# Delta-rule attention feeding a mixture of softmax attentions: scores and maxima as paired 64-row products

## The chip, the cores and the metric

The kernel runs on one core of one Trainium2 chip. The metric is the device time of one execution in microseconds. Three timed runs of the kernel before gave 500.80, 500.83 and 502.74 us, median 500.83. A separate execution was recorded by the profiler.

## The reference, cut to what matters

Inputs: q, k, v of shape 4 x 8 x 768 x 48 (batch, head, position, feature), beta, and weights for 4 experts with 64 features each. A first stage runs a delta rule over the positions of each batch and head:

```python
k_n = k / (norm(k) + 1e-6)
for t in range(768):
    y[t] = q[t] @ state
    state += beta[t] * outer(k_n[t], v[t] - k_n[t] @ state)
```

Its output, 4 x 768 x 384, is the input x of a causal softmax attention per expert, mixed with gates of the two best experts per position:

```python
for e in range(4):
    s = where(causal, -1e9, (x @ wq[e]) @ (x @ wk[e]).T / 8)
    a = exp(s - s.max(-1)); a /= a.sum(-1) + 1e-9
    out += gate[e] * (a @ (x @ wv[e]) @ wo[e])
```

## The kernel before, in words

The 768 positions are cut into three parts of 256, and the four batches into two pairs, which gives six stages n = 0..5: stages 0, 1, 2 walk along one pair of batches, 3, 4, 5 along the other. `s = n % 3` is the part. A stage has four chunks c of 64 positions, with 16 batch-head pairs side by side.

The delta rule of a stage is solved blockwise. `gram` (L214) forms products of the keys of a chunk; `solve_pre` and `solve_step` (L266, L311) invert triangular blocks of 32, or of 16 in stage 0, on VectorE (DVE) for stage 0 and on GpSimd (POOL) for the others, framed by the transposes of `st_in`, `st_out` and `st_nat`; the `merge` functions widen the blocks to 64. Then the chunks go one after another through `chain_ks`, `chain_u`, `chain_s`, `chain_q` and `chain_y` (L427 to L474). Their products are small and packed into quadrants of the array: the list `by` sorts the 16 pairs so that consecutive products use different row halves (r = 0 or 64) and column halves. `chain_q` (L459) reads rows r and writes partitions r; `chain_y` (L467) reads rows v and writes partitions r, where v is r or 64-r.

For the attention, `proj_qk` (L487) makes queries and keys of 128 positions for a pair of batches. Values are split into a high part, rounded to the type fp32r, and a low part with the rest. The tiles of 128 rows are laid out so that one product does two things. In `KA`, the half that belongs to a head's parity has the high part of the keys, the other half the low part; `QA` has the queries' high part in both halves. `KA * QA` is then khi*qhi + klo*qhi. In `KH`, one half has the keys' high part again, and eight rows of the other half hold -1 where a row belongs to expert e (`pick_rows`, L417); `QL` has the queries' low part and, in those eight rows, the row maxima (`max_rows`, L609). `KH * QL` is khi*qlo - max. For this each projection is copied out of PSUM by four ScalarE (ACT) copies of 64 x 512 (L508 and L511, or L508 and L514) and two DVE subtractions of 64 x 512 (L517 or L519).

`max_list` (L567) has units of one expert, or of two of the same parity: a product over up to 512 keys, a mask product in bf16 with an identity where the diagonal is reached, and a DVE maximum out of PSUM (L589). A score unit (`score`, L624) is one expert and two key blocks of 128: two products per block over 256 queries (128 for the last block of the diagonal), masks where kp = s, and exponentials on ACT into a tile of the pool `at` of five. `av` (L644) multiplies these with the values in column halves, into one of two places in the bank `PO`; ACT copies the 64 features and the row sum separately (L658, L659). `norm`, `fin_t` and `fin_o` scale, transpose and multiply with wo.

PSUM has eight banks: `po` one (also used by the filler), `xu` two, `py` two, and a ring of three named `pm_` for everything else.

What sets the order of the work is `ORDER` (L36), a list of steps that is played back as it stands; each engine's queue then runs in that order and waits on semaphores. `+39` in it is 39 fillers: products of 252 columns on a zero tile (L118) that keep TensorE busy. All loads, the spreading of rows (L480) and the stores are issued from SyncE (SP), in the same order. In the names of steps, gr is `gram`, gq `gram_q`, si `st_in`, pre and sv the solve, pj `proj_qk`, mx, mp and mr the maximum and its rows, sc `score`.

## Time and profile before

| what | value |
|---|---|
| median of three runs | 500.83 us |
| the profiled execution, whole | 500.28 us |
| its span, first to last instruction | 498.6 us |
| mean granted TensorE clock | 0.969 |
| instructions | 24842 |
| products on TensorE, each with its weight load | 11169 |
| the loading DMA queue's share of 16 DMA engines | 20.0% |

PE is TensorE's products, PEld its weight loads, which run beside them. Rows of the timeline give start, duration, engine, line, operation and tiles. `KA,QA` at L109 is a maximum's product, `QA,KA` and `QL,KH` are a score's; `mbias,identb` is a mask, `po<-zb` a filler. L109 is the line of the helper that issues every product. Rows that group instructions give count, busy time, mean duration in ns, and the idle time ahead of them with what ended it.

### The profile page before, as it was taken

How to read it: one execution, taken by the hardware profiler on the slowest of the kernel's cores; microseconds unless marked ns; L12 is line 12 of the kernel's file. 1: busy time of each engine (PE TensorE's matmuls, PEld its weight loads, DVE VectorE, ACT ScalarE, POOL GpSimd, SP SyncE). 2: the span in 40 equal slices, each digit the busy share in tenths (PEclk: the TensorE clock that was granted, in tenths of full speed). 3: DMA queues.
4: the chain of work that ended last, by engine and by line, in shares of the span. 5: the costliest groups of instructions: out<-in, count | busy, mean ns of one | idle time of the engine just before them, and what ended most of it. 6: DMA issues, size and time to landing. Idle time of an engine off the chain costs nothing.

```text
span 498.6 us, 24842 instructions
## 1 busy us (share of the span) xinstructions
PE 468.2 (94%) x11169; PEld 415.2 (83%) x11169; DVE 298.0 (60%) x661; ACT 264.0 (53%) x659; POOL 228.5 (46%) x382
## 2 busy tenths in 40 slices
PE   8998767899999999998989999999999999999997
PEld 6687657798899878887978899998898979988896
DVE  0479502246895887473797667676756863357522
ACT  3112352348566445645464556674566664773563
POOL 7101088683008885788711778625987020000000
PEclk9699975999999999999999999999999999999999
DMA  8500020424132210135301123013220112000002
GB/s 270 194 5 1 5 79 8 146 67 141 36 103 79 67 47 18 64 92 183 92 3 58 58 67 101 6 41 112 69 67 17 50 35 83 20 2 32 3 17 80
DMA packets 18825, 32.63 MB, mean 65 GB/s; under 512 B 2848, under 2 KB 8864, under 8 KB 18720
## 3 DMA queue, kind: packets, MB, share of 16 engines
q1 hardware_dynamic: 18720, 31.04, 20.0%
q8 instruction: 88, 1.44, 1.2%
q14 instruction: 17, 0.14, 0.1%
HBM read 23.96 MB, written 4.72 MB: 58 GB/s over the span
## 4 chain that ended last, share of the span: by engine, by line
PE 77%; DVE 10%; issue 5%; ACT 3%; SPq 3%; DMA 2%; ACTq 0%; DVEq 0%
PE po L109 15%; PE xu L109 7%; PE py L109 6%; SPq L480 2%; DVE mx L589 1%; DVE tt L346 1%; DMA xh<-h 1%; DVE tn L343 1%; DVE B L248 1%; DVE B L245 1%; DMA kf<-in_kq_dram 1%; DVE KA L517 1%; DVE QL L519 1%; ACT QA L511 0%; PE pm__3152 L109 0%
## 5 line engine op out<-in xcount | busy, mean ns | idle before, releaser
L324 POOL TENSOR_TENSOR B<-B,tm 128x30 f32<-128x30 f32 (+9 forms) x150 | 79.6, 530 | 11.8
L323 POOL TENSOR_TENSOR tm<-B 128x30 f32<-128x30 f32 (+9 forms) x150 | 73.7, 492 | 10.7
L109 PE MATMUL po<-zb 128*128 128x252 bf16 x385 | 53.3, 288 | 3.0 <-issue 1.4
L109 PE MATMUL po<-VS,at 128*64 128x65 f32 x1344 | 49.8, 226 | 0.1
L109 PEld LDWEIGHTS po<-VS,at 128*64 128x64 f32 x1344 | 43.1, 138 | 5.8 <-issue 1.9
L109 PEld LDWEIGHTS <-zb 128*128 128x128 bf16 x385 | 36.8, 102 | 10.3 <-issue 2.5
L141 POOL TENSOR_TENSOR kv<-kv,nt 128x384 f32<-128x384 f32 x24 | 19.9, 830 | 48.8 <-DMA kv<-in_kv_dram 19.3
L397 POOL MEMSET tt<- 32x1024 f32 x10 | 9.4, 944 | 50.1 <-PE pm__7779 L109 12.7
L658 ACT ACTIVATE os<-po 128x128 f32<-128x128 f32 x48 | 13.3, 278 | 26.8 <-PE po L109 26.5
L109 PEld LDWEIGHTS <-identb 128*128 128x128 bf16 x192 | 18.4, 96 | 7.6 <-issue 2.0
L109 PE MATMUL py<-qf,sb 48*48 48x64 f32 x704 | 24.6, 222 | 0.0
L301 POOL TENSOR_TENSOR B<-B,nn 128x1024 f32<-128x1024 f32 x5 | 11.8, 2369 | 27.7 <-DVE nn L300 27.7
L109 PEld LDWEIGHTS py<-qf,sb 48*48 48x48 f32 x704 | 21.8, 123 | 1.4 <-issue 0.4
L473 DVE TENSOR_TENSOR xh<-py,xh 112x384 fp32r<-112x384 f32 x24 | 13.4, 557 | 15.9 <-ACT h L472 15.7
L434 DVE TENSOR_TENSOR xs<-kv,xu 128x384 f32<-128x384 f32 x22 | 12.1, 551 | 15.8 <-PE xu L109 12.0
L471 ACT ACTIVATE xh<-py 112x384 fp32r<-112x384 f32 x24 | 11.8, 491 | 16.9 <-PE py L109 16.7
L452 DVE TENSOR_TENSOR sb<-sb,xu 112x384 f32<-112x384 f32 x20 | 11.0, 551 | 16.1 <-ACT at L639 7.3
L248 DVE STREAM_TRANSPOSE B<-tt 32x1024 f32<-32x1024 f32 x10 | 20.0, 2001 | 0.2
L440 ACT ACTIVATE ub<-xu 128x384 f32<-128x384 f32 x24 | 11.8, 490 | 13.6 <-PE xu L109 11.2
L109 PE MATMUL xu<-xs,tt 64*64 64x48 f32 x768 | 17.6, 225 | 1.4 <-issue 0.9
L109 PEld LDWEIGHTS xu<-xs,tt 64*64 64x64 f32 x768 | 14.6, 138 | 3.8 <-issue 1.7
L109 PE MATMUL py<-pm,ub 64*48 64x64 f32 x768 | 16.0, 221 | 0.6 <-issue 0.6
(2055 smaller groups left out, 1446.8 us busy)
## 6 DMA issues: line engine op xcount, KB each, us to landing
kv<-in_kv_dram SPq DMA_DIRECT2D x24, 384.0 KB, 3.6
kf<-in_kq_dram SPq DMA_DIRECT2D x24, 256.0 KB, 3.7
qf<-in_kq_dram SPq DMA_DIRECT2D x24, 256.0 KB, 3.7
out_dram<-ot SPq DMA_DIRECT2D x24, 192.0 KB, 1.9
xh<-h SPq DMA_DIRECT2D x72, 32.0 KB, 2.0
wst<-in_wqk_dram SPq DMA_DIRECT2D x3, 256.0 KB, 5.2
wst<-in_wvg_dram SPq DMA_DIRECT2D x1, 256.0 KB, 5.3
wst<-in_wo_dram SPq DMA_DIRECT2D x1, 256.0 KB, 3.5
```

Of the source, the lines that this page charges most:

```text
L109: T.matmul(o, lhsT=a, rhs=b, start=start, stop=stop, skip_group_check=True)
L141: G.tensor_tensor(vt, vt, PR[n]["nt"][:, c * NP:c * NP + NP, None].to_broadcast([128, NP, HD]), op=OP.mult)
L248: V.transpose(B[r:r + 32], gf[r:r + 32, :, 0:32].rearrange("p t j -> p j t"))
L301: G.tensor_tensor(pr["B"], pr["B"], nn[:, None, :].to_broadcast([128, 32, 32]), op=OP.mult)
L323: e.tensor_tensor(tv, bc(Z[:, i:i + 1, i + 1:]), bc(Z[:, 0:i, i:i + 1]), op=OP.mult)
L324: e.tensor_tensor(Z[:, 0:i, i + 1:], Z[:, 0:i, i + 1:], tv, op=OP.add)
L434: V.tensor_tensor(eight(XB), eight(vt), PX, op=OP.subtract)
L440: S.activation(eight(UB), PX, AF.Copy)
L452: V.tensor_tensor(eight(new), eight(state(n, c)), SP, op=OP.add)
L471: S.activation(hi, Y[:, :, 0:3], AF.Copy)
L473: V.tensor_tensor(lo, Y[:, :, 0:3], hi, op=OP.subtract)
L658: S.activation(os[:, :, e], O[:, :, 0:EH], AF.Copy)
```

## The change

Heads go through scores and maxima two at a time. `KHI`, `KLO`, `QHI` and `QLO` hold two experts in the two halves of the 128 rows, as they come out of the projection, so a projection takes one ACT copy and one DVE subtraction of 128 x 512. Every product of scores and maxima has 64 rows, and products of the two heads are issued in turn, each into a bank of its own. A score is khi*qhi + khi*qlo + klo*qhi and a fourth product of `SEL` (-1 in the rows of expert e) with `MR` (the row maxima); the maximum is taken of khi*qhi alone. Masks are two products of 64 rows per head. `score` and the units of the maximum take a pair of experts (y) and two banks, so there are half as many units.

The bank `po` is gone: fillers write to the unused half of a `py` bank, now with 256 columns, `av` takes a bank of the ring, and the ring has four banks (`bufs=4` wherever it had 3). `av` copies features and row sums at once, and `norm` writes to a new tile. The pool `at` has seven tiles (`ATB`). The queries have two buffers. The constants grow from 504 to 1012 columns and come in three DMAs instead of two. `ORDER` is a new list, with 250 fillers in place of 384. In the old one 88 fillers stand ahead of gr0.0, the last of the four gr0 steps, which si0 follows; in the new one all four gr0 steps come within 52 fillers, and si0 right behind them.

```diff
@@ ORDER, the first line of each
-+39 gr0.2 sq3 sq0 sq2 +12 gr0.1 +5 sr0 lc0.1 sq1 sr2 gr1.2 +3 sr1 +6 gq0.1 sr3 pre0.0 pre0.1 +1 gr1.0 pre0.2 w0 pre0.3
...
+sq1 +22 gr0.0 +9 gr0.2 sq2 +21 gr0.3 gr0.1 si0 lc0.1 sq3 sr1 gr1.1 sr2 sq0 +7 sr0 sr3 pre0.0 pre0.1 pre0.2 pre0.3
...
@@ -112,11 +104,11 @@
 
     ZB = cp.tile([128, 256], BF16, name="zb")
     V.memset(ZB, 0.0)
-    PO = ps.tile([128, 512], F32, name="po")
-    mm(PO[:, 260:512], ZB[:, 0:128], ZB[:, 0:252], True)
+    PY0 = ps.tile([128, 2, 512], F32, name="py")
+    mm(PY0[:, 0, 256:512], ZB[:, 0:128], ZB, True)
 
     def filler():
-        mm(PO[:, 260:512], ZB[:, 0:128], ZB[:, 0:252], False)
+        mm(PY0[:, 0, 256:512], ZB[:, 0:128], ZB, False)
 
     KR = [cp.tile([128, NP, 64], F32, name=f"kf{i}") for i in range(KB)]
     QR = [cp.tile([128, NP, 64], F32, name=f"qf{i}") for i in range(QB)]
...
@@ -144,18 +136,19 @@
 
     VS = cp.tile([128, 2, 6, NE, EH + 1], F32, name="VS")
     KF = VS.rearrange("p a b c d -> p (a b c d)")
-    cst = cp.tile([128, 240], F32, name="cst")
+    cst = cp.tile([128, 500], F32, name="cst")
     bta = cp.tile([128, NU, 32], F32, name="bta")
-    csb = wk.tile([128, 264], F32, name="csb", tag="at", bufs=5)
+    csb = wk.tile([128, 512], F32, name="csb", tag="at", bufs=ATB)
     load_k(0, 0)
-    nc.sync.dma_start(cst, consts[:, 0:240])
+    nc.sync.dma_start(cst[:, 0:240], consts[:, 0:240])
...
@@ -164,12 +157,15 @@
     pmask = cst[:, 128:192]
     lower = cst[:, 192:208]
     kmask = cst[:, 208:240]
-    identb = cp.tile([128, 128], BF16, name="identb")
-    mbias = cp.tile([128, 2, 128], BF16, name="mbias")
+    identb = cp.tile([128, 2, 128], BF16, name="identb")
+    mbias = cp.tile([128, 2, 2, 128], BF16, name="mbias")
     TG = [cp.tile([128, NT, 64], F32, name=f"tt{i}") for i in range(2)]
-    KA = cp.tile([128, NE, 2, NS], F32R, name="KA")
-    QL = cp.tile([128, NE, 2, 256], F32R, name="QL")
-    KH = cp.tile([128, NE, 2, NS], F32R, name="KH")
+
+
+    KHI = cp.tile([128, 2, 2, NS], F32R, name="KHI")
+    KLO = cp.tile([128, 2, 2, NS], F32R, name="KLO")
+    MR = cp.tile([128, 2, 2, 256], F32R, name="MR")
+    SEL = cp.tile([128, NE, 128], F32R, name="SEL")
 
     slot = lambda k, h: KF[:, 260 * k + 256 * h:260 * k + 256 * h + 256].rearrange("p (t i) -> p t i", t=NP)
     GO = [[slot(k, h) for k in ks for h in range(2)] for ks in ((0, 8), (4, 10))]
@@ -178,9 +174,8 @@
         G.memset(GO[0][c], 0.0)
     for t in AS + GO[1]:
         G.memset(t, 0.0)
-    for r, x in HA:
-        G.memset(QL[64 - r:128 - r, x::2].bitcast(F32), 0.0)
-        G.memset(KH[64 - r:128 - r, x::2].bitcast(F32), 0.0)
+    G.memset(SEL.bitcast(F32), 0.0)
+    G.memset(MR.bitcast(F32), 0.0)
 
     wqkh = cp.tile([128, 3, 512], F32R, name="wqkh")
     wqkl = cp.tile([128, 3, 512], F32R, name="wqkl")
...
@@ -411,14 +406,11 @@
         for w in LB:
             for r, _ in HA:
                 S.activation(w[r:r + 32, 0], ident[r:r + 32, r:r + 32], AF.Copy)
-        S.activation(identb, ident, AF.Copy)
-        S.activation(mbias.rearrange("p a b -> p (a b)"), csb[:, 0:256], AF.Copy)
+        S.activation(identb, cst[:, 240:496].rearrange("p (a b) -> p a b", a=2), AF.Copy)
+        S.activation(mbias.rearrange("p a h b -> p (a h b)"), csb, AF.Copy)
 
     def pick_rows(r, e):
-        S.activation(KH[64 - r:72 - r, e].rearrange("p b t -> p (b t)"),
-                     csb[64 - r:72 - r, 256 + e:257 + e].to_broadcast([8, 2 * NS]), AF.Copy)
-
-
+        S.activation(SEL[r:r + 8, e], cst[r:r + 8, 496 + e:497 + e].to_broadcast([8, 128]), AF.Copy)
 
     XH = {}
     first_of = lambda n, c: n % 3 == 0 and c == 0
@@ -488,10 +480,10 @@
         s = n % 3
         y, isk = m % 2, m // 2
         if n not in QT:
-            QT[n] = (wk.tile([128, NE, 2, 256], F32R, name="QA", bufs=1), QL)
+            QT[n] = tuple(wk.tile([128, 2, 2, 256], F32R, name=x, bufs=2) for x in ("QHI", "QLO"))
         xh = XH[n, hb][0]
         if y == 0:
-            PQ[0] = ps.tile([128, 2, 2, 128], F32, name="pm_", bufs=3)
+            PQ[0] = ps.tile([128, 2, 2, 128], F32, name="pm_", bufs=4)
         P = PQ[0]
         w = slice(128 * m, 128 * m + 128)
         j = 0
@@ -501,22 +493,10 @@
                 j += 1
         if y == 0:
             return
-        qa, ql = QT[n]
-        hs = [(slice(64 * x, 64 * x + 64), slice(64 - 64 * x, 128 - 64 * x), slice(x, NE, 2)) for x in range(2)]
+        hi, lo = (KHI, KLO) if isk else QT[n]
         t = slice(256 * s + 128 * hb, 256 * s + 128 * hb + 128) if isk else slice(128 * hb, 128 * hb + 128)
-        for h, _, es in hs:
-            S.activation((KA if isk else qa)[h, es, :, t], P[h], AF.Copy)
-        if not isk:
-            for h, o, es in hs:
-                S.activation(qa[o, es, :, t], P[h], AF.Copy)
-        else:
-            for h, _, es in hs:
-                S.activation(KH[h, es, :, t], P[h], AF.Copy)
-        for h, o, es in hs:
-            if isk:
-                V.tensor_tensor(KA[o, es, :, t], P[h], KA[h, es, :, t], op=OP.subtract)
-            else:
-                V.tensor_tensor(ql[h, es, :, t], P[h], qa[h, es, :, t], op=OP.subtract)
+        S.activation(hi[:, :, :, t], P, AF.Copy)
+        V.tensor_tensor(lo[:, :, :, t], P, hi[:, :, :, t], op=OP.subtract)
 
     def ones(k):
         G.memset(VS[:, :, 2 * k:2 * k + 2, :, EH:], 1.0)
...
@@ -572,29 +552,30 @@
         L = []
         st = {}
 
-        def one(k0, nb, x, y, per, sec):
+        def one(k0, nb, y, per, sec):
             if n not in MX:
                 MX[n] = wk.tile([128, 2, 2, NE], F32, name="mx")
             if sec and "m2" not in st:
                 st["m2"] = wk.tile([128, NE], F32, name="mx2")
             dst = st["m2"] if sec else MX[n][:, i, b]
             dg = k0 + nb == nk
-            P = ps.tile([128, per, 128 * nb], F32, name="pm_", bufs=3)
+            P = [ps.tile([128, per, 128 * nb], F32, name="pm_", bufs=4) for _ in HA]
             for j in range(per):
-                e = 2 * (y + j) + x
-                mm(P[:, j], QT[n][0][:, e, b, 128 * i:128 * i + 128], KA[:, e, b, 128 * k0:128 * (k0 + nb)], True,
-                   not dg)
-                if dg:
-                    mm(P[:, j, 128 * (nb - 1):], identb, mbias[:, 0], False)
-            V.tensor_reduce(dst.rearrange("p (y x) -> p x y", x=2)[:, x, y:y + per], P, axis=AX.X, op=OP.max)
+                for r, x in HA:
+                    mm(P[x][:, j], QT[n][0][r:r + 64, y + j, b, 128 * i:128 * i + 128],
+                       KHI[r:r + 64, y + j, b, 128 * k0:128 * (k0 + nb)], True, not dg)
+                for h in range(2 * dg):
+                    for r, x in HA:
+                        mm(P[x][:, j, 128 * (nb - 1):], identb[r:r + 64, h], mbias[r:r + 64, 0, h], False, h == 1)
+            for _, x in HA:
+                V.tensor_reduce(dst.rearrange("p (y x) -> p x y", x=2)[:, x, y:y + per], P[x], axis=AX.X, op=OP.max)
 
         for k0, nb, sec in ((0, main, False), (4, rest, True)):
             if not nb:
                 continue
             per = 2 if nb <= 2 else 1
-            for x in range(2):
-                for y in range(0, 2, per):
-                    L.append(lambda k0=k0, nb=nb, x=x, y=y, per=per, sec=sec: one(k0, nb, x, y, per, sec))
+            for y in range(0, 2, per):
+                L.append(lambda k0=k0, nb=nb, y=y, per=per, sec=sec: one(k0, nb, y, per, sec))
         if rest:
             L.append(lambda: V.tensor_tensor(MX[n][:, i, b], MX[n][:, i, b], st["m2"], op=OP.max))
         return L
@@ -609,67 +590,70 @@
     def max_rows(n, b):
 
         mp = MX[n, b].bitcast(F32)
-        P = ps.tile([8, 2, 128], F32, name="pm_", bufs=3)
+        P = ps.tile([8, 2, 128], F32, name="pm_", bufs=4)
         for i in range(2):
             T.transpose(P[:, i], mp[:, i].rearrange("p a b -> p (a b)"), ident)
+        S.activation(MR[0:8, n % 2, b], P.rearrange("p i t -> p (i t)"), AF.Copy)
+        S.activation(MR[64:72, n % 2, b], P.rearrange("p i t -> p (i t)"), AF.Copy)
+
+    AT, OS = {}, {}
+
+    def score(n, b, y, kp):
+        s = n % 3
+        A, P = [], []
         for r, x in HA:
-            o, p = QL[64 - r:72 - r, x::2, b], P.rearrange("p i t -> p (i t)")[:, None, :].to_broadcast([8, 2, 256])
-            if x:
-                V.tensor_copy(o, p)
-            else:
-                S.activation(o, p, AF.Copy)
-
-    AT, OS, OC = {}, {}, []
-
-    def score(n, b, e, kp):
-        s = n % 3
-        A = AT[n, b, e, kp] = wk.tile([128, 2, 256], F32, name="at", tag="at", bufs=5)
-        qa, ql = QT[n]
-        P = ps.tile([128, 2, 256], F32, name="pm_", bufs=3)
+            t = wk.tile([128, 2, 256], F32, name="at", tag="at", bufs=ATB)
+            AT[n, b, 2 * y + x, kp] = t
+            A.append(t)
+            P.append(ps.tile([128, 2, 256], F32, name="pm_", bufs=4))
+        qh, ql = QT[n]
+        dg = kp == s
         for j in range(2):
             kb = 2 * kp + j
             q0 = 128 if kb == 2 * s + 1 else 0
-            dg = kp == s
             ks = slice(128 * kb, 128 * kb + 128)
-            mm(P[:, j, q0:], KA[:, e, b, ks], qa[:, e, b, q0:], True, False)
-            mm(P[:, j, q0:], KH[:, e, b, ks], ql[:, e, b, q0:], False, not dg)
-            if dg:
-                mm(P[:, j, 128 * j:128 * j + 128], identb, mbias[:, 1], False)
-        if kp < s:
-            S.activation(A, P, AF.Exp, scale=0.125)
-        else:
-            S.activation(A[:, 0], P[:, 0], AF.Exp, scale=0.125)
-            S.activation(A[:, 1, 128:], P[:, 1, 128:], AF.Exp, scale=0.125)
+            for k, (a, q) in enumerate(((KHI, qh), (KHI, ql), (KLO, qh))):
+                for r, x in HA:
+                    mm(P[x][:, j, q0:], a[r:r + 64, y, b, ks], q[r:r + 64, y, b, q0:], k == 0, False)
+            for r, x in HA:
+                mm(P[x][:, j, q0:], SEL[r:r + 64, 2 * y + x], MR[r:r + 64, n % 2, b, q0:], False, not dg)
+            for h in range(2 * dg):
+                for r, x in HA:
+                    mm(P[x][:, j, 128 * j:128 * j + 128], identb[r:r + 64, h], mbias[r:r + 64, 1, h], False, h == 1)
+        for _, x in HA:
+            if kp < s:
+                S.activation(A[x], P[x], AF.Exp, scale=0.125)
+            else:
+                S.activation(A[x][:, 0], P[x][:, 0], AF.Exp, scale=0.125)
+                S.activation(A[x][:, 1, 128:], P[x][:, 1, 128:], AF.Exp, scale=0.125)
 
     def av(n, b, e):
         s = n % 3
         if (n, b) not in OS:
-            OS[n, b] = (wk.tile([128, 2, NE, EH], F32, name="os", bufs=2), wk.tile([128, 2, NE], F32, name="rs", bufs=2))
-        o = 2 * (EH + 1) * (len(OC) % 2)
-        OC.append(0)
-        O = PO[:, o:o + 2 * (EH + 1)].rearrange("p (i d) -> p i d", i=2)
+            OS[n, b] = wk.tile([128, 2, NE, EH + 1], F32, name="os", bufs=2)
+        O = ps.tile([128, 2, EH + 1], F32, name="pm_", bufs=4)
         for i in range(2):
             for kb in range(2 * s + i + 1):
                 for j in range(2):
                     q0 = 128 * i + 64 * j
                     mm(O[64 * j:64 * j + 64, i], AT[n, b, e, kb // 2][:, kb % 2, q0:q0 + 64], VS[:, b, kb, e], i == 0 and kb == 0,
                        kb == 2 * s + i)
-        os, rs = OS[n, b]
-        S.activation(os[:, :, e], O[:, :, 0:EH], AF.Copy)
-        S.activation(rs[:, :, e], O[:, :, EH], AF.Copy)
+        S.activation(OS[n, b][:, :, e], O, AF.Copy)
 
     def norm(n, b):
-        os, rs = OS[n, b]
-        V.tensor_scalar(rs, rs, 1e-9, None, op0=OP.add)
+        rs = wk.tile([128, 2, NE], F32, name="rs", bufs=1)
+        os = OS[n, b]
+        V.tensor_scalar(rs, os[:, :, :, EH], 1e-9, None, op0=OP.add)
         V.reciprocal(rs, rs)
         V.tensor_tensor(rs, rs, GT[n][:, 2 * b:2 * b + 2], op=OP.mult)
-        V.tensor_tensor(os, os, rs[:, :, :, None].to_broadcast([128, 2, NE, EH]), op=OP.mult)
+        OS[n, b] = wk.tile([128, 2, NE, EH], F32, name="on", bufs=2)
+        V.tensor_tensor(OS[n, b], os[:, :, :, 0:EH], rs[:, :, :, None].to_broadcast([128, 2, NE, EH]), op=OP.mult)
 
     OH = {}
 
     def fin_t(n, b):
-        os = OS[n, b][0]
-        P = ps.tile([128, 2, 2, 128], F32, name="pm_", bufs=3)
+        os = OS[n, b]
+        P = ps.tile([128, 2, 2, 128], F32, name="pm_", bufs=4)
         for i in range(2):
             for x in range(2):
                 T.transpose(P[:, i, x], os[:, i, 2 * x:2 * x + 2].rearrange("p e d -> p (e d)"), ident)
...
```

More of the change, by code (lines that the diff above doesn't have):

```diff
@@ L215, in gram @@
         gf, x = PR[n]["gf"], LD[n, c]
-        g = [ps.tile([128, 4, 64], F32, name="pm_", bufs=3) for _ in range(2)]
+        g = [ps.tile([128, 4, 64], F32, name="pm_", bufs=4) for _ in range(2)]
         for p, i, _, r, t, _ in by(1):
@@ L236, in gram_q @@
         pm = PR[n]["pm", c] = wk.tile([128, NP, 64], F32, name="pm", bufs=PB)
-        g = [ps.tile([128, 4, 64], F32, name="pm_", bufs=3) for _ in range(2)]
+        g = [ps.tile([128, 4, 64], F32, name="pm_", bufs=4) for _ in range(2)]
         for p, _, _, r, _, v in by(0):
@@ L369, in merge1 @@
         gf, m = TG[n % 2], NP if n < NL else 16
-        W = ps.tile([128, m, 32], F32, name="pm_", bufs=3)
+        W = ps.tile([128, m, 32], F32, name="pm_", bufs=4)
         for i in range(m):
@@ L381, in merge2 @@
         ws, o = lanes(n), TG[n % 2][:, NP * c:NP * c + NP]
[L382 removed]
+        W = ps.tile([128, NP, 64], F32, name="pm_", bufs=4)
         for i in range(NP):
@@ L402, in tile_kernel @@
     XS = ps.tile([128, 2, 512], F32, name="xu")
-    YY = ps.tile([112, 2, 512], F32, name="py")
+    YY = PY0[0:112]
     four = lambda t: t.rearrange("p f (i e) -> p f i e", i=4)
@@ L528, in proj_v @@
         xh = XH[n, hb][0]
-        P = ps.tile([128, 260], F32, name="pm_", bufs=3)
+        P = ps.tile([128, 260], F32, name="pm_", bufs=4)
         j = 0
@@ L684, in fin_o @@
         oh, ol = OH[n, b]
-        R = ps.tile([128, DM], F32, name="pm_", bufs=3)
+        R = ps.tile([128, DM], F32, name="pm_", bufs=4)
         j = 0
@@ L740, in tile_kernel @@
                 step("av", av, n, b, e)
+            for y in range(2):
                 for kp in range(n % 3 + 1):
-                    step("sc", score, n, b, e, kp)
+                    step("sc", score, n, b, y, kp)
             for i in range(2):
@@ L794, in _layout @@
     c[:, 208:240] = ((i % 32)[:, None] >= np.arange(32)) & ((i % 32 // 16)[:, None] == np.arange(32) // 16)
-    c[:, 240:368] = np.where(i[None, :] > i[:, None], NEG, 0.0)
-    c[:, 368:496] = np.where(i[:, None] > i[None, :], NEG, 0.0)
-    for x in (0, 1):
-        c[64 - 64 * x:72 - 64 * x, 496:500] = -np.tile(np.eye(4), (2, 1))
+    m0 = np.where(i[None, :] > i[:, None], NEG, 0.0)
+    for x in (0, 64):
+        c[x:x + 64, 240:752] = np.stack([m0, m0.T]).reshape(2, 2, 64, 128).transpose(2, 0, 1, 3).reshape(64, 512)
+        c[x:x + 64, 752:1008] = np.eye(128).reshape(2, 64, 128).transpose(1, 0, 2).reshape(64, 256)
+        c[x:x + 8, 1008:1012] = -np.tile(np.eye(4), (2, 1))
     a["consts"] = c
```

118 lines of the change are left out of this document (55 added, 63 removed).

## The prediction

> **What bounds the kernel now.** I read the page first, then the stretches table, then the timeline of the attention units.
>
> ```profile
> span 498.6 us, 24842 instructions
> PE 468.2 (94%) x11169; PEld 415.2 (83%) x11169; DVE 298.0 (60%) x661; ACT 264.0 (53%) x659; POOL 228.5 (46%) x382
> PE 77%; DVE 10%; issue 5%; ACT 3%; SPq 3%; DMA 2%; ACTq 0%; DVEq 0%
> L109 PE MATMUL po<-zb 128*128 128x252 bf16 x385 | 53.3, 288 | 3.0 <-issue 1.4 <-DVE on L162 1.1 <-ACT rs L659 0.4
> ```
>
> TensorE is busy 94% of the span and carries 77% of the chain that ended last. The last row corrects that: 385 of its products are fillers on a zero tile, 53 us of the 468. Where they stand is told by two stretches, first of everything, then of the filler's tile alone:
>
> ```profile
> 0.00:110.00 110.00, 92.38 (x2958) 77.97 (x2958) 47.07 (x126) 36.79 (x89) 53.86 (x94) 0.88 0.27 87
> 110.00:498.60 388.60, 375.81 (x8219) 337.25 (x8211) 250.97 (x536) 227.22 (x570) 174.64 (x289) 1.00 0.20 59
> ```
> ```profile
> 110.00:498.60 388.60, 12.40 (x87) 7.94 (x87) 0.00 (x0) 0.00 (x0) 1.00 0.20 59
> ```
>
> The columns after the length are PE, PEld, DVE, ACT, POOL. Behind 110 us TensorE has 376 of 389 us, of which only 12 are filler, while DVE has 251, ACT 227 and POOL 175. So there are two regimes: a start that waits on a chain of steps, and from 110 us on a kernel paced by TensorE, where whatever comes off TensorE's work comes off the time, and what comes off ACT and DVE does not.
>
> **The attention products now.** Products of one maximum unit (two heads, 256 keys, a mask each), then a score unit off the diagonal; ahead of them 32 products of another kind:
>
> ```profile
> 275.02 1.06 PE L109 MATMUL py<-qf,sb 48*48 48x64 f32 x32
> 276.01 0.39 PE L109 MATMUL pm__5358<-KA,QA 128*128 128x256 f32 x1
> 276.24 0.23 PE L109 MATMUL pm__5358<-mbias,identb 128*128 128x128 bf16 x1
> 276.28 0.36 PE L109 MATMUL pm__5358<-KA,QA 128*128 128x256 f32 x1
> 276.48 0.23 PE L109 MATMUL pm__5358<-mbias,identb 128*128 128x128 bf16 x1
> 276.52 0.36 PE L109 MATMUL pm__5365<-QA,KA 128*128 128x256 f32 x1
> 276.72 0.28 PE L109 MATMUL pm__5365<-QL,KH 128*128 128x256 f32 x1
> 276.84 0.28 PE L109 MATMUL pm__5365<-QA,KA 128*128 128x256 f32 x1
> 276.96 0.28 PE L109 MATMUL pm__5365<-QL,KH 128*128 128x256 f32 x1
> ```
>
> Durations contain latency; what a product costs is the step to the next start. The maximum unit takes 276.52-276.01 = 0.51 us. In the score unit the steps are 0.20, 0.12, 0.12 and, by the same pace, 0.12: 0.56 us, of which 0.08 is a weight load that nothing hid at the unit's start. A diagonal score unit, and maxima over 512 keys:
>
> ```profile
> 462.44 0.38 PE L109 MATMUL pm__8865<-QA,KA 128*128 128x256 f32 x1
> 462.66 0.28 PE L109 MATMUL pm__8865<-QL,KH 128*128 128x256 f32 x1
> 462.78 0.23 PE L109 MATMUL pm__8865<-mbias,identb 128*128 128x128 bf16 x1
> 462.82 0.31 PE L109 MATMUL pm__8865<-QA,KA 128*128 128x128 f32 x1
> 462.96 0.27 PE L109 MATMUL pm__8865<-QL,KH 128*128 128x128 f32 x1
> 463.08 0.23 PE L109 MATMUL pm__8865<-mbias,identb 128*128 128x128 bf16 x1
> 463.12 0.36 PE L109 MATMUL pm__8875<-QA,KA 128*128 128x256 f32 x1
> ```
> ```profile
> 269.40 0.50 PE L109 MATMUL pm__5209<-KA,QA 128*128 128x512 f32 x1
> 269.74 0.40 PE L109 MATMUL pm__5213<-KA,QA 128*128 128x512 f32 x1
> ```
>
> The diagonal unit takes 463.12-462.44 = 0.68 us. A 512-key product with an uncovered start takes 0.34, so a start costs 0.08 to 0.10 over the 0.24 of twice 256 columns. A 128-key product still takes 0.12 to 0.14, so a product costs the longer of its load (about 0.12 for 128 columns) and its stream (0.12 per 256 columns). Counting the loops: 48 diagonal and 48 other score units, 48*0.68+48*0.56 = 59.5 us; 96 maximum units between 0.34 and 0.51, taken at 0.39 (a third of them are the 512-key kind without a mask), 37.4 us. Together 97 us.
>
> **The pair of halves.** After the change a head has four 64-row products per key block where it had two of 128 rows (khi*qhi, khi*qlo, klo*qhi, and the row that subtracts the maximum): 768 products, not 384. They are issued as pairs, one head in rows 0-63, one in 64-127, 384 rounds. Maxima stay 128 products but drop to 64 rounds. All hangs on what a round costs, and no row shows two 64-row products over all 128 columns. The nearest rows are these, with the 275.02 row:
>
> ```profile
> 281.98 0.63 PE L109 MATMUL py<-pm,ub 64*48 64x64 f32 x32
> 282.43 0.23 PE L109 MATMUL pm__5493<-qf,kf 48*64 48x64 f32 x2
> ```
> ```profile
> 276.72 0.19 PEld L109 LDWEIGHTS pm__5365<-QA,KA 128*128 128x128 f32 x1
> 276.84 0.19 PEld L109 LDWEIGHTS pm__5365<-QL,KH 128*128 128x128 f32 x1
> ```
>
> Both groups of 32 load 48 columns and stream 64. The first (L459) uses two quadrants of the array, rows and columns both different, and takes (276.01-275.02)/32 = 31 ns a product, 62 for two. The second (L467) goes round four quadrants, so both row halves load and stream over the same columns, and takes (282.43-281.98)/32 = 14 ns a product, 56 for four. Adding the other row half under the same columns costs nothing. So I take a round at the price of one product, 0.12 us; the upper bound is two turns, 0.24. Below 0.12 it can't fall, since one head's load alone takes that.
>
> The Trainium skill (TensorE: Matmul & The Clock Gate, "What overlaps and what doesn't") speaks against the change: a weight load overlaps a running product only when the row group differs, so each half would wait for its own product. The PEld rows above disagree for full-height products: a 0.19 us load starts together with the product at 276.72, and another with the one at 276.84, on the same rows. What the rule would do here is the second rival below.
>
> **The sum.** A pair unit off the diagonal: 8 rounds*0.12+0.08 = 1.04 us, 24 of them, 25.0. On the diagonal: four rounds at 0.12 with the 0.10 of a start, two mask rounds at 0.04, four rounds of 0.12 with 0.02 for coming back from a mask, two more masks: 1.24 us, 24 of them, 29.8. Maxima: 48 units at 0.39 plus 0.04 for the second mask half, 20.6. Together 75.4 against 97: **-21.5 us on TensorE**. Half of it is the maximum's halved rounds, the rest starts that are paid once per pair. Bounds: -12 if every bank of a pair brings an uncovered start of its own; +32 at two turns a round (448 rounds*0.12 = 54 more).
>
> Evictions and normalisation:
>
> ```profile
> 229.01 1.20 ACT L508 ACTIVATE QA<-pm__4521 64x512 fp32r<-64x512 f32 x2 [1.61 <-PE pm__4521 L109]
> 230.22 1.19 ACT L511 ACTIVATE QA<-pm__4521 64x512 fp32r<-64x512 f32 x2
> ```
> ```profile
> 231.44 1.39 DVE L519 TENSOR_TENSOR QL<-pm__4521,QA 64x512 fp32r<-64x512 f32 x2 [4.38 <-ACT QA L511]
> ```
> ```profile
> 466.49 0.60 ACT L639 ACTIVATE at<-pm__8916 128x512 f32<-128x512 f32 x1 [0.61 <-PE pm__8916 L109]
> ```
> ```profile
> L659 ACT ACTIVATE rs<-po 128x2 f32<-128x2 f32 x48 | 8.2, 170 | 0.0
> ```
>
> A projection loses three of four copies and one of two subtractions. A 128x512 copy costs 0.60, so ACT loses 24*(2.39-0.60) = 43 us and, with the row sums of L659, 51; DVE loses 24*0.69 = 17. That is off the path behind 110 us; I count 0. The bound is the 2.5 us by which each of the 24 projections is ready earlier, covered now by other products; uncovered it would show as TensorE idle, of which that stretch holds 388.6-375.8 = 13 us in all. The smaller MR and SEL writes, the strided norm, the smaller memsets on POOL and the larger constants (one more DMA on SP's queue ahead of the four query loads) are costed at 0: none feeds TensorE in the first 16 us except through those loads, and the first use of queries stands behind 59 fillers.
>
> The start, from the chain in order of time and the timeline of DVE:
>
> ```profile
> 28.36 1.98 DVE B L245
> ...
> 30.44 1.30 DVE B L298
> ```
> ```profile
> 25.42 0.19 DVE L292 TENSOR_TENSOR aa<-nn,bta 128x32 f32<-128x32 f32 x1
> ```
>
> The first solve starts when both the transposed Gram block (30.34) and the scale aa (25.61) are there. The Gram block is late because gr0.0 is issued last, behind 88 fillers. The new order issues all four gr0 after 52 and si0 right behind, so aa becomes the later one: 30.44-25.61 = **-4.8 us**, of which I take 4.5. Bounds 0 and -8 (si1's transposes also move behind the first merge).
>
> DMA waits elsewhere move with the order; the largest on the chain is this, so I allow 3 us either way:
>
> ```profile
> 222.48 3.30 DMA kf<-in_kq_dram
> ```
>
> The plan's fillers fall from 384 to 250, mostly at the start, counted above; behind 110 us 87 become 27, which is worth 0, since they stood in waits, to -8 at 12.40/87 = 0.14 us each. The sum is made on the profiled run's own 500.3 us (1.7 outside the span), 0.1% under the median of 500.83. 500.3-21.5-4.5 = **474 us**.
>
> **Rivals.**
> *Banks.* A score unit now needs two of four banks free at once, AV takes from the same ring, and its accumulators no longer have a bank of their own. If each of the 48 score units waited for one more exponential (0.60), 29 us return: 503, no change. Against it: ACT falls from 227 to about 180 of 389 us, and AV or chain work usually stands between units. For it: seven `at` buffers, six of them held by one head pair at three key pairs. In part, it gives 488 to 498.
> *Load behind its own half's product.* A round becomes load plus stream, 0.12+0.12 for 256 columns and 0.12+0.06 for 128: 288*0.12+96*0.06+64*0.12 = 48 us more, 522. The PEld rows speak against it.
> *Turns.* This one ends slower: if the halves with 128 columns, or fp32r products of 64 rows, don't run side by side, 448 rounds cost 0.12 more and the time is 474+54 = 528. It decides from a round of 0.12+26/448 = 0.18 us on: above that the kernel is slower than before. For it: every packed group in the trace is at most 64 columns wide and plain f32. The Trainium skill (TensorE: Matmul & The Clock Gate, "LDWEIGHTS") prices a load by its columns alone, so 64 rows would save nothing on each of two loads.
>
> **Numbers.** Forecast 0.67, its own range 462 to 488; banks 0.15 (0.08 still faster, 0.05 no change, 0.02 slower, since the 48 maximum units can wait as well); load behind product 0.06; turns 0.12. The predicted time is 474. From 462 to 508 leaves out the last two rivals and 0.02 below. A measurement here can tell about 0.5%: faster 0.67+0.08 = 0.75, same 0.05, slower 0.20.
>
> **What would show it.** Right: pairs of KHI products starting together, rounds 0.12 us apart, score and maximum units adding to about 75 us; the first solve stepping from 27 us instead of 30.44+1.30 = 31.7; fewer than 15 us of TensorE idle behind 105 us. Wrong: starts within a pair 0.12 apart (turns), rounds of 0.24 within one half (loads), or rounds of 0.12 with gaps of 0.6 ahead of units, ended by exponentials (banks).

## The result and the profile after

| | before | after |
|---|---|---|
| median of the timed runs (4 each) | 500.95 us | 481.49 us |
| profiled execution / its span | 500.28 / 498.6 us | 481.12 / 479.4 us |
| mean granted TensorE clock | 0.969 | 0.950 |

The ratio is 0.9604, 95% interval 0.9572 to 0.9636. The kernel is 19.5 us faster. The prediction was 474 us, from terms of 26.0 us: the direction and the range held, and some 7 us of the gain are missing (6.5 by the terms, 7.5 by the time). The rest of this document is about those 7 us.

The page of the changed kernel, then the two stretches (columns as before: PE, PEld, DVE, ACT, POOL, granted clock), then the filler's tile alone:

```profile
span 479.4 us, 25556 instructions
PE 445.7 (93%) x11611; PEld 396.5 (83%) x11611; DVE 274.9 (57%) x625; ACT 211.3 (44%) x551; POOL 223.3 (47%) x380
PE 64%; DVE 4%; SPq 1%; issue 1%; DMA 1%; ACT 1%; DVEq 0%; ACTq 0%
L101 PE MATMUL py<-zb 128*128 128x256 bf16 x251 | 37.2, 302 | 4.3 <-DVE h L466 2.1
```
```profile
0.00:110.00 110.00, 89.74 (x2899) 77.23 (x2900) 53.19 (x130) 31.34 (x86) 50.99 (x93) 0.84 0.31 99
110.00:479.40 369.40, 355.91 (x8714) 319.31 (x8713) 221.66 (x496) 179.94 (x465) 172.28 (x287) 0.98 0.20 60
```
```profile
110.00:479.40 369.40, 5.06 (x27) 2.32 (x27) 0.00 (x0) 0.00 (x0) 0.98 0.20 60
```

TensorE still paces the second stretch: 13.5 us idle in 369.4, 5 of its 356 us filler. ACT fell as forecast (264 to 211 us, 51 forecast), DVE by more (298 to 275, 17 forecast). New is the clock: 0.98 behind 110 us, where it was 1.00.

A maximum unit of two heads and 256 keys, then a plain one over 512 keys, a filler, and a score unit off the diagonal; behind them the first weight loads of the score unit:

```profile
440.45 0.38 PE L101 MATMUL pm__9092<-KHI,QHI 64*128 64x256 f32 x1
440.45 0.38 PE L101 MATMUL pm__9093<-KHI,QHI 64*128 64x256 f32 x1
440.68 0.23 PE L101 MATMUL pm__9092<-mbias,identb 64*128 64x128 bf16 x1
...
440.77 0.36 PE L101 MATMUL pm__9092<-KHI,QHI 64*128 64x256 f32 x1
...
441.19 1.50 PE L101 MATMUL pm__9109<-VS,at 128*64 128x65 f32 x44
442.62 0.49 PE L101 MATMUL pm__9133<-KHI,QHI 64*128 64x512 f32 x1
...
443.05 0.28 PE L101 MATMUL py<-zb 128*128 128x256 bf16 x1
443.27 0.39 PE L101 MATMUL pm__9142<-QHI,KHI 64*128 64x256 f32 x1
443.27 0.39 PE L101 MATMUL pm__9144<-QHI,KHI 64*128 64x256 f32 x1
443.49 0.27 PE L101 MATMUL pm__9142<-QLO,KHI 64*128 64x256 f32 x1
443.50 0.27 PE L101 MATMUL pm__9144<-QLO,KHI 64*128 64x256 f32 x1
443.61 0.28 PE L101 MATMUL pm__9142<-QHI,KLO 64*128 64x256 f32 x1
...
444.19 0.28 PE L101 MATMUL pm__9142<-MR,SEL 64*128 64x256 f32 x1
...
444.40 0.28 PE L101 MATMUL pm__9163<-VS,at 128*64 128x65 f32 x2
```
```profile
443.26 0.18 PEld L101 LDWEIGHTS pm__9142<-QHI,KHI 64*128 64x128 f32 x1
443.37 0.19 PEld L101 LDWEIGHTS pm__9142<-QLO,KHI 64*128 64x128 f32 x1
```

The two heads start together, and rounds follow at 0.12 us: two 64-row products cost what one 128-row product costs. But at each end of a unit, where the height of the products changes, a step takes 0.21 to 0.22 instead of 0.12 (443.27 to 443.49 and 444.19 to 444.40): the weight load there is covered by nothing. Inside the unit a load starts 0.12 ahead of its product (443.37 for 443.49), at its entry only together with it (443.26 for 443.27). The 512-key unit takes 0.43, where the kernel before took 0.34 for its product of 128 rows.

Adding up, for all products from the first projection of queries or keys on, the time to the next product's start (what lies between the end of all earlier products and the next start is counted as idle), in us:

| | first projection starts | scores and maxima | projections | Gram, merge | chain | AV | output | filler | idle | last product ends |
|---|---|---|---|---|---|---|---|---|---|---|
| before | 99.1 | 97.6 | 81.0 | 50.5 | 61.5 | 46.5 | 36.1 | 13.0 | 9.3 | 495.1 |
| after | 93.4 | 85.3 | 84.5 | 52.6 | 62.7 | 44.6 | 37.0 | 4.4 | 11.0 | 475.9 |
| difference | -5.7 | -12.3 | +3.5 | +2.1 | +1.2 | -1.9 | +0.9 | -8.6 | +1.7 | -19.2 |

Projections, Gram and chain products are the same in both kernels, and yet they take 7 us more. 1.8 of that is only where the count starts: in the kernel before, nine value products and 32 Gram products stand ahead of the first projection of queries or keys (its first value product starts at 96.4), in the changed kernel behind it. 3.6 is the clock, by the share of the clock withheld while these products ran; the rest, most of it in the projections, was not taken apart. In scores and maxima the clock took 1.9 us of the 85.3.

In windows of 3.4 us, the sum of (1 - granted clock) * 3.4 behind 95 us is 2.1 us before and 7.4 after. The last window reaches past the last instruction (0.5 of the 2.1, 0.6 of the 7.4); the other 6.8 us lie in two dips, near 210 and 250 us, where the kernel before has one of 1.7, near 262.

### The profile page after: what moved, and what is told of

It is laid out like the page before. It is cut to its first block, busy times and chain, and to the rows that moved or that the text cites. A ratio compares the mean times of both kernels' runs of the same rounds, so it can differ in the third digit from the quotient of the medians.

```text
span 479.4 us, 25556 instructions
## 1 busy us (share of the span) xinstructions
PE 445.7 (93%) x11611; PEld 396.5 (83%) x11611; DVE 274.9 (57%) x625; ACT 211.3 (44%) x551; POOL 223.3 (47%) x380
## 3 DMA queue, kind: packets, MB, share of 16 engines
q8 instruction: 91, 1.49, 1.3%
## 4 chain that ended last, share of the span: by engine, by line
PE 64%; DVE 4%; SPq 1%; issue 1%; DMA 1%; ACT 1%; DVEq 0%; ACTq 0%
PE xu L101 6%; PE py L101 6%; SPq L472 1%; DMA xh<-h 1%; DVE B L243 1%; PE pm__4861 L101 0%; PE pm__5871 L101 0%; PE pm__8461 L101 0%; PE pm__7776 L101 0%; PE pm__8849 L101 0%; PE pm__7418 L101 0%; PE pm__8799 L101 0%; PE pm__3084 L101 0%; PE pm__2995 L101 0%; PE pm__6357 L101 0%
## 5 line engine op out<-in xcount | busy, mean ns | idle before, releaser
L101 PE MATMUL py<-zb 128*128 128x256 bf16 x251 | 37.2, 302 | 4.3 <-DVE h L466 2.1
L101 PEld LDWEIGHTS <-zb 128*128 128x128 bf16 x251 | 25.6, 107 | 9.8 <-issue 2.4
L296 POOL TENSOR_TENSOR B<-B,nn 128x1024 f32<-128x1024 f32 x5 | 11.8, 2363 | 25.6 <-DVE nn L295 20.7
L101 PE MATMUL xu<-ub,kv 64*48 64x48 f32 x704 | 14.2, 216 | 1.4 <-issue 1.2
L101 PEld LDWEIGHTS xu<-sb,kf 48*64 48x64 f32 x704 | 12.5, 137 | 3.2 <-issue 1.1
L101 PE MATMUL xu<-sb,kf 48*64 48x48 f32 x704 | 15.1, 224 | 0.1
L101 PEld LDWEIGHTS <-identb 64*128 64x128 bf16 x384 | 12.2, 96 | 3.6 <-issue 0.5
```

The source lines that it names most:

```text
L101: T.matmul(o, lhsT=a, rhs=b, start=start, stop=stop, skip_group_check=True)
L296: G.tensor_tensor(pr["B"], pr["B"], nn[:, None, :].to_broadcast([128, 32, 32]), op=OP.mult)
```

## Experiments

Times are medians; "before" is the kernel before on the same chip, whose medians lay between 499.2 and 500.4 us in what follows.

**The changed kernel again**, as yardstick.

> The changed kernel once more, unaltered, on the chip of the two kernels sent with it, as the yardstick for differences under 1%. All theories: 478 to 483 us; if the two half-clock dips behind 110 us belong to the order of the work, the profile shows them again near 210 and 250 us.

481.45 us, ratio to before 0.9618 (0.9581 to 0.9655). Its profile has both dips again, and again 7.4 us of clock lost behind 95 us, so they are no accident of one execution. The first projection starts at 94.6 here, at 93.4 in the first profile: differences of a microsecond in the start can't be told.

**One head after the other, key block by key block.**

```diff
-            for k, (a, q) in enumerate(((KHI, qh), (KHI, ql), (KLO, qh))):
-                for r, x in HA:
+            for r, x in HA:
+                for k, (a, q) in enumerate(((KHI, qh), (KHI, ql), (KLO, qh))):
...
```

> Same products, banks, evictions and order of steps as the changed kernel; only inside a score unit the four products (and masks) of one head are issued before those of the other, key block by key block. Theory (halves run side by side only where neighbours in the order sit in different halves): in a key block 8 products take 7 turns instead of 4, so 96 blocks x 3 x 0.115 = +33 us, with the masks some +36, about 517 us. Turns theory (a pair never ran side by side, the gain is from somewhere else): no change, 481. A rival on the queue (TensorE itself pairs what stands in its queue): no change either, and the products of the two heads would still start together.

481.36 us, ratio 0.9615 (0.9528 to 0.9701): no change in the time. From its timeline, the start of a unit on the diagonal:

```profile
459.36 0.38 PE L101 MATMUL pm__9469<-QHI,KHI 64*128 64x256 f32 x1
459.70 0.28 PE L101 MATMUL pm__9469<-QHI,KLO 64*128 64x256 f32 x1
459.71 0.39 PE L101 MATMUL pm__9471<-QHI,KHI 64*128 64x256 f32 x1
```

The second head's first product starts beside the first head's third, not behind its sixth: the third theory was right in the main. But the two heads no longer start together, and by the count of the table scores and maxima take 92.4 us, 7 more than in the changed kernel. The time does not show it: the idle time is 7.7 for 11.0, and the dip near 250 us is 3.4 us long instead of 10.2.

**One head after the other, unit by unit.**

```diff
-        for j in range(2):
+        for r, x in HA:
+            for j in range(2):
...
```

> All products of a score unit for one head, both key blocks, then all of the other head: 8 products (12 with the masks) of one half stand ahead of the first of the other. With one key block at a time the other half had started about four products ahead of its turn, which hid the reordering. Theory A (TensorE looks ahead some four products and no further): 4 to 8 rounds a unit are lost, 24 x 4 x 0.115 + 24 x 8 x 0.09 = +28 us, about 510. Theory B (it looks ahead over its whole queue): no change, 481 to 483.

498.97 us, ratio 1.0004 (0.9967 to 1.0041). With nothing changed but the order of products within a score unit, 17.5 us are lost: without the halves running side by side there is no gain. That the time comes out at that of the kernel before is chance; scores and maxima cost 17 us more than there, and the other parts of the change pay that back. From this kernel's timeline, a unit on the diagonal near its middle:

```profile
471.13 0.27 PE L101 MATMUL pm__9358<-QLO,KHI 64*128 64x128 f32 x1
471.25 0.27 PE L101 MATMUL pm__9358<-QHI,KLO 64*128 64x128 f32 x1
471.25 0.38 PE L101 MATMUL pm__9360<-QHI,KHI 64*128 64x256 f32 x1
471.36 0.27 PE L101 MATMUL pm__9358<-MR,SEL 64*128 64x128 f32 x1
471.48 0.23 PE L101 MATMUL pm__9358<-mbias,identb 64*128 64x128 bf16 x1
471.48 0.28 PE L101 MATMUL pm__9360<-QLO,KHI 64*128 64x256 f32 x1
471.54 0.22 PE L101 MATMUL pm__9358<-mbias,identb 64*128 64x128 bf16 x1
```

In the program all products into bank 9358 stand ahead of the first into 9360. That one starts at 471.25, with three of 9358's still to start and a fourth starting beside it. So TensorE takes products of the other half ahead of their turn, by four places here and no further: in 47 of the kernel's 48 score units three products of the first half start after the other half's first, in one four. With one key block at a time, runs of 4 to 6 products, this hides most of the reordering. The Trainium skill (TensorE: Matmul & The Clock Gate, "What overlaps and what doesn't") has products start in strict program order; these rows disagree.

By the same count as in the table, scores and maxima take 114.4 us here, 29 more than in the changed kernel, as theory A had it (28). The time rises by 17.5 only: no dip comes in this kernel (0.8 us of clock lost, all behind the last instruction) and the idle time falls from 11.0 to 5.8.

**Masks at full height.**

```diff
...
-            for h in range(2 * dg):
-                for r, x in HA:
-                    mm(P[x][:, j, 128 * j:128 * j + 128], identb[r:r + 64, h], mbias[r:r + 64, 1, h], False, h == 1)
+            if dg:
+                for r, x in HA:
+                    mm(P[x][:, j, 128 * j:128 * j + 128], identb, mbias[:, 1], False)
...
```

The same is done in the maxima, with an identity and masks of 128 rows.

> The masks are added as products of 128 rows again (one for each head, identity of 128 rows) in place of two halves for each head, inside units whose other products have 64 rows. 96 blocks carry a mask. Theory A (what was mis-sized is the second mask half): two full products at 0.04 take the place of two rounds that last 0.09 together, 0 to -3 us, about 479. Theory B (each change between full height and half height leaves a weight load uncovered, 0.09 us): each masked block gets two changes more, 96 x (0.18 + 0.08 - 0.09) = +16 us, about 497.

483.64 us, ratio 0.9656 (0.9563 to 0.975). Its timeline in a diagonal unit, one bank's rows:

```profile
457.29 0.28 PE L101 MATMUL pm__9175<-MR,SEL 64*128 64x256 f32 x1
...
457.50 0.23 PE L101 MATMUL pm__9175<-mbias,identb 128*128 128x128 bf16 x1
457.56 0.22 PE L101 MATMUL pm__9177<-mbias,identb 128*128 128x128 bf16 x1
457.71 0.33 PE L101 MATMUL pm__9175<-QHI,KHI 64*128 64x128 f32 x1
```

Into the full-height masks 0.21, out of them 0.15: theory B's mechanism. Scores and maxima take 99.3 us, 14 more than in the changed kernel, near B's 16. But the time rises by 2 us, inside what can be told. Again the dip near 250 us is missing (4.1 us of clock lost) and the idle time is 5.0. So neither theory gives the time: of the 14 us, the idle time took up 6.0, and projections, Gram and chain products take 4.3 us less than in the changed kernel, at less clock lost. That this room is there for any work added is not shown.

**Without the product of the maximum.**

```diff
-            for r, x in HA:
-                mm(P[x][:, j, q0:], SEL[r:r + 64, 2 * y + x], MR[r:r + 64, n % 2, b, q0:], False, not dg)
...
```

> Leaves out the product that subtracts the row's maximum from the scores (so the exponentials are taken of unshifted scores); the maxima are still formed. 96 rounds fewer on TensorE, nothing less on ACT and DVE. Theory (TensorE paces behind 110 us, a round costs 0.115): -11 us, about 470.5. Rival (banks and exponentials pace the units): 480 to 482.

466.83 us, ratio 0.934 (0.9267 to 0.9413): 14.7 us less. Scores and maxima take 73.6 us, 11.7 less, or 0.12 for each of 96 rounds; 2.9 us less clock is lost, and the first projection starts 1.4 us earlier, which nothing in the edit explains. Here taking work off TensorE paid in full, where adding work cost little. With the same dip near 250 us absent, this is consistent with the clock, but why the two directions differ so much is not settled.

**Four copies for each projection.**

```diff
-        S.activation(hi[:, :, :, t], P, AF.Copy)
-        V.tensor_tensor(lo[:, :, :, t], P, hi[:, :, :, t], op=OP.subtract)
+        for r, _ in HA:
+            S.activation(X4[0:64], P[r:r + 64], AF.Copy)
+            S.activation(hi[r:r + 64, :, :, t], P[r:r + 64], AF.Copy)
+        for r, _ in HA:
+            V.tensor_tensor(lo[r:r + 64, :, :, t], P[r:r + 64], hi[r:r + 64, :, :, t], op=OP.subtract)
...
```

> One part undone in cost: each of the 24 projections leaves its bank by four copies of 64 rows (two of them to a scratch tile) and two subtractions, as many instructions as in the kernel before. ACT gets about 1.8 us more for each, 43 in all, DVE 0.7 more, 17 in all. Forecast (off the path behind 110 us): 481 to 484. Rival (a projection that is ready later holds up its units): up to 24 x 2.5 = 60 us more, 500 to 541.

520.66 us, ratio 1.0428 (1.0333 to 1.0523): 39 us more. Its page, and what TensorE waited for:

```profile
PE 466.5 (90%) x11611; PEld 413.3 (80%) x11611; DVE 292.5 (56%) x649; ACT 251.0 (48%) x623; POOL 222.8 (43%) x380
```
```profile
PE pm__8937 L101 <- DVE QLO L503: 2.0, 1, 2.0
PE pm__8633 L101 <- DVE KLO L503: 1.8, 1, 1.8
```

ACT works 40 us more, at 48% of the span, and is nobody's bound by its share. Yet TensorE waits for the projection's last reader, the subtraction (L503), before it may use the bank again: both products shown are maxima, which read neither `QLO` nor `KLO`. Behind the first projection such waits come to 10 us, and waits for a copy (L501) that maxima read themselves to 5. Idle rises from 11.0 to 28.6 us, and the clock falls to 0.94 behind 95 us: 28.2 us of it are lost, for 7.4. So about 18 of the 39 us are idle time and some 20 are clock; that the waits bring the dips is not shown. An eviction is not off the path when the ring of banks waits for it. The order was made for the short eviction; that a new order would win some of this back was not tried.

**Three banks.**

```diff
-name="pm_", bufs=4
+name="pm_", bufs=3
...
```

The same in all twelve places that take from the ring.

> The ring of the changed kernel with three banks in place of four, nothing else. Theory A (the fourth bank is slack: behind the first projection TensorE idles only 11 us): +0 to +5 us, 481 to 487. Theory B (the prediction's rival on banks: a pair that needs two banks waits for one more exponential or maximum): 96 units x 0.6 = +58 us, about 540. What four copies for a projection cost (39 us, most of it TensorE waiting for a bank's last reader) speaks for B.

525.87 us, ratio 1.0557 (1.0478 to 1.0635): 44 us more, nearer to B. Idle is 28.0 us, of which waits for exponentials (L625, L628) are 10.7 and for maxima (L571) 5.0; scores and maxima take 101.7 with the waits between the two banks of a pair, and the first projection starts 9 us later. The rival on banks is a real mechanism; the fourth bank, from the old `po`, is what keeps it away.

**Fillers ahead of the two dips.**

```diff
-... hx2.1.0 u2.2 q2.2 ... m13.1 pre4.0 pre4.1 m13.0 vt3.0 cl3 gq4.0 ...
+... hx2.1.0 +10 u2.2 q2.2 ... m13.1 pre4.0 pre4.1 +6 m13.0 vt3.0 cl3 +6 gq4.0 ...
```

> 22 fillers more, ahead of the two stretches behind 110 us in which the granted clock was half: ten where TensorE waits for the chain near 207 us, twelve between the merge products and Gram products near 244 us. Theory A (thin or absent work on TensorE brings the clock down, and the two dips cost 1.7 and 5.1 us of full clock): about -6.8 + 12 x 0.12 = -5, some 476. Theory B (the dips don't follow TensorE's work, or the time lost in them is hidden): 481 to 484.

478.75 us, ratio 0.9586 (0.9531 to 0.9641): not to be told from the changed kernel. The dip near 250 is gone, the one near 210 is larger (3.3 us, for 1.7 in the changed kernel). Inconclusive.

**The start: weights later, queries later.** The stall that this is about, and the same in the stage of small products behind 50 us, from the timeline of the changed kernel (start, duration, then the idle time before it, for which the profile shows no releaser), and the feed's own row on its page:

```profile
18.16 0.26 PE L101 MATMUL pm__380<-kf 48*64 48x64 f32 x1 [3.42 <-issue]
...
50.73 0.58 PE L101 MATMUL pm__951<-tt,VS 32*32 32x16 f32 x47 [0.85 <-issue]
54.82 0.21 PE L101 MATMUL pm__1057<-B,tn 32*32 32x64 f32 x1 [1.31 <-issue]
58.38 0.27 PE L101 MATMUL pm__1091<-VS,tn 32*32 32x16 f32 x4 [2.05 <-issue]
61.83 0.27 PE L101 MATMUL pm__1194<-VS,tn 32*32 32x16 f32 x4 [1.51 <-issue]
```
```profile
q8 instruction: 91, 1.49, 1.3%
q14 instruction: 16, 0.13, 0.1%
```

These stalls stand behind product 348, 1112, 1239, 1367, 1495: 127 or 128 apart, or a multiple. 1.62 MB for 25556 instructions are 63 bytes each, and a packet of 1.49 MB/91 = 16.4 KB holds 256 of them, 128 products with their loads. In the trace, packets of this queue (16,384 bytes) have landed at 16.7, 49.5, 53.4, 56.9 and 60.4 us, and each stall ends 1.2 to 1.5 us after one. So TensorE waits for its next packet of instructions. The Trainium skill (Runtime: NRT & Kernel Launch, "Instruction fetch mechanics") has the fetch in lines of 16 KiB, which agrees, and hidden behind the issue of instructions, which these rows contradict.

```diff
-        st = wk.tile([128, 512], F32, name="wst", tag="at", bufs=ATB)
+        st = wk.tile([128, 512], F32, name="wst", bufs=2)
```

> The seven weight pieces are loaded through two buffers of their own in place of seven shared ones, so that five of the loads start later. In the changed kernel TensorE stands still for 3.42 us in the middle of a Gram (from 14.74 us) with nothing to wait for but its instructions, while the data loads keep the DMA engines full until 20 us. Theory A (the instructions come late because of the loads): the stall shrinks to under 1 us, the sums of squares are read at 21 instead of 23.3 us, the first solve steps from about 27.5, the end comes 2 us earlier, 479. Theory B (the stall has another cause): no change, 481.

477.44 us, ratio 0.9591 (0.9548 to 0.9633). The stall is there still:

```profile
18.48 0.26 PE L101 MATMUL pm__380<-kf 48*64 48x64 f32 x1 [3.71 <-issue]
```

The ratio is not to be told from the changed kernel's, and the start gave nothing: the first projection starts at 95.0, for 93.4 and 94.6 in the two profiles of the changed kernel.

```diff
-    for c in range(CH):
-        load_q(0, c)
...
+        if x == "lc0.1":
+            for c in range(CH):
+                G.tensor_copy(QR[c][:, 0, 0:1], TG[0][:, 8 * c, 0:1])
+                load_q(0, c)
```

> The four first query loads and, behind them on SP's queue, the weight pieces start only when the first Gram blocks have been copied out (about 14.5 us instead of 8.8): each query tile gets one element written by POOL from a Gram block first. The stall of TensorE stands behind its 348th product, and the next ones about 128 products apart, so it waits for its instructions there. Theory A (the feed is late because the data loads fill the DMA engines from 5 to 20 us): the stall of 3.42 us falls under 1 us, the sums of squares are read at 20 instead of 23.3 us, the first solve steps from 26.5 instead of 29.9; the end 0 to 3 us earlier, 478 to 481. Theory B (the feed is slow by itself): the stall stays over 2.5 us, no change.

477.42 us, ratio 0.9553 (0.9516 to 0.9589), at the edge of what can be told from the yardstick's 0.9618.

```profile
16.85 0.26 PE L101 MATMUL pm__384<-kf 48*64 48x64 f32 x1 [2.34 <-issue]
```
```profile
23.28 1.29 DVE L272 SCALAR_TENSOR_TENSOR g<-g,rr 128x32 f32<-128x32 f32 x1
```

Nearer to B: 2.34 us, against 3.42 in the changed kernel's first profile and 2.69 in the yardstick's on the same chip. The sums are read at 22.0, 1.1 earlier than in the yardstick, but the first solve steps at 29.67, as there (29.69): one DVE instruction between them took 1.29 us here and 0.19 there. The first projection starts at 94.5. Most of the stall is the feed's own. What gain there is lies behind the first projection: 3.9 us of clock lost, 9.0 idle.

**All three together**: both load edits, and the twelve fillers ahead of the merge.

> Queries later, the weights through two buffers of their own, and the twelve fillers ahead of the merge at 244 us, all in one. If each is worth what its profile lets hope (start 2 to 3 us, dip 2 to 3 us): 475 to 477, against 481 for the changed kernel. If the start's gain is lost again in the stage of small products behind 50 us, which the feed of instructions paces: 478 to 480.

474.59 us, ratio 0.9489 (0.9458 to 0.9521), the fastest kernel here, 6.9 us under the yardstick on the same chip. The stretches of the two dips, first in the changed kernel, then here:

```profile
200.00:220.00 20.00, 17.36 (x554) 15.30 (x546) 11.56 (x28) 8.84 (x25) 18.12 (x29) 0.91 0.43 129
240.00:260.00 20.00, 19.27 (x384) 17.02 (x384) 13.12 (x33) 8.57 (x17) 5.70 (x7) 0.74 0.08 26
```
```profile
200.00:220.00 20.00, 17.63 (x600) 15.63 (x599) 12.03 (x30) 10.05 (x27) 18.04 (x30) 1.00 0.41 119
240.00:260.00 20.00, 20.00 (x532) 17.12 (x534) 16.00 (x41) 12.01 (x25) 8.45 (x14) 1.00 0.15 46
```

TensorE is as busy, but at a clock of 0.74 it gets 384 products done in the second stretch, at 1.00 it gets 532 (not all of one kind). Behind 95 us 0.1 us of clock is lost, and 8.3 us are idle. The start gave nothing: the first projection starts at 95.3, for 94.6 in the yardstick, and the end comes 6.1 us earlier than in the first profile all the same. So with no dip in its trace this order takes 474.6. Its six executions took 473.5 to 481.2 us, at mean clocks from 0.967 down to 0.938, and one was traced; that the dips stay away every time is not shown. Which of the three edits keeps them away was not taken apart.

## Why the prediction was right, and 7 us short

- **Two regimes, TensorE paces the second.** Right as far as it went: 13.5 us of idle behind 110 us, and 96 rounds fewer gave 14.7 us. But it is not a rule of one for one: 14 us more (masks) cost 2, 29 more (one head after the other) cost 17.5, since idle time and the clock lost changed with them.
- **A round of two 64-row products at 0.12.** Right: 0.115 to 0.12. "Load behind its own half's product" (0.18 to 0.24) and "turns" fell on the first timeline, and the kernel with whole units in turn shows part of what turns would have cost (29 us more for scores and maxima, with four places still overlapping). The rows of `chain_q` and `chain_y` were good evidence. The rule of the Trainium skill weighed there (a load waits for a running product of its own rows; TensorE: Matmul & The Clock Gate, "What overlaps and what doesn't") does not hold within a half. Where the height changes, a load is left uncovered (0.21 instead of 0.12).
- **The sum, -21.5 us.** This is the step that failed. The side of before was right (97 forecast, 97.6 measured), the side of after not: 75.4 forecast, 85.3 measured. Most of it is the term "48*(0.39+0.04)" for the maxima: a unit takes 0.56 on average and all take 27.0 us, not 20.6. A plain 512-key unit takes 0.43 instead of 0.34, since it is entered and left with an uncovered load, where before its neighbours of full height covered one of them. And the two rounds of a mask in halves take 0.09 a key block (440.68 to 440.77), where I counted 0.04 more a unit. The score units were 0.04 to 0.05 too low each (medians of 1.28 on the diagonal and 1.09 off it, for 1.24 and 1.04), and with a few slow ones 3.5 us in all. The dips are 1.9 of the 10 us; in the kernel with all three edits, which has none, scores and maxima still take 83.7. I had taken the cost of a start from products that enter a unit, and none for leaving it.
- **Evictions counted 0.** As forecast, ACT's and DVE's share tells nothing of a gain. But the reason given ("off the path") does not hold for this order: undone, the time rises by 39 us, through waits on the ring of banks and a lower clock. That the pairs need shorter evictions to work with four banks in any order is not shown.
- **Start, -4.5.** Measured -5.7 by the first projection of queries or keys, but -3.0 by the first of any kind (96.4 to 93.4), since the old order has a value projection first; and not by the step forecast. The Gram block was early, as said (its transpose starts at 14.50), and `aa` did become the later one. But it was not ready at 25.6: the sums of squares stand behind product 348, and TensorE stands still there for 3.42 us.

```profile
14.50 1.92 DVE L240 STREAM_TRANSPOSE B<-tt 128x1024 f32<-128x1024 f32 x1
23.33 0.19 DVE L259 COPY ss<-xu 128x32 f32<-128x32 f32 x1 [6.91 <-PE xu L101]
...
29.90 0.19 DVE L321 TENSOR_TENSOR tm<-B 128x28 f32<-128x28 f32 x1
```

  The first solve steps at 29.90, 1.9 us earlier than before (31.77), not at 27. The assumption that a step's time stays what it was when the steps ahead of it are changed was the fault.
- **Fillers worth 0.** Behind the first projection they fell from 13.0 to 4.4 us, a gain of 8.6, just past the bound that I gave (0 to -8, behind 110 us). It was taken back: +5.3 us of clock lost and +1.7 us of idle. That fewer fillers let the clock fall is not shown: the dip near 250 us stayed away in seven kernels, and five of them (masks at full height, no maximum row, three banks, whole units in turn, queries later) had no filler more.
- **Together**: -12.3 for -21.5, start -5.7 for -4.5, fillers and AV -10.5 for 0, and +9.4 for 0 on idle time and work that did not change. Of the 9.4, 3.2 are the clock, 1.8 where the count starts and 1.7 idle; 2.7 were not taken apart. The kernel without dips, at 474.6, is where the forecast was, but by errors that cancel: the maxima too cheap, the fillers too worthless.
- **Banks**, the likeliest rival, did not come: no wait on an exponential stands among TensorE's. With three banks it did (10.7 us).

## What to carry to other kernels

Products that use half the rows pay when they are issued as neighbours of the other half; TensorE reached four places ahead here, so runs of 4 to 6 cost no time (though 7 us of TensorE's), and runs of 8 to 12 cost 17.5. Count a change of height at both ends of such a unit (0.09 us each here), and keep units of one height together. When work comes off the bounding engine, look at its clock before and after: here two dips, absent from the trace after a small shift of loads and fillers, came to about as much as the forecast was short.
